# Attention and feed-forward on one core: another hand-written order of the first 28 steps, with GpSimd in it, ten low parts on GpSimd, and first loads from ScalarE's queue

## Chip, cores and metric

One core of one Trainium2 chip. The metric is device time in microseconds (us) of one execution; for the kernel before, the median of three runs is 829.32 us (828.08 to 829.99).

## What is computed

```python
# q, k, v: [8 batches, 8 heads, 576, 64] f32; w_in [512, 2048], w_out [2048, 512] f32
scores = (q @ k^T) / 8
# heads 0-3: key 0..31 places back; heads 4-7: every 4th key, 0..124 places back
attn = softmax(where(mask, scores, -1e9))
x = (attn @ v)  ->  [4608 tokens, 512]
h = x @ w_in
out = (h * clip(h + 3, 0, 6) / 6) @ w_out
```

All of it is float32. For the feed-forward part every operand is split in two: a high part, rounded to the format that TensorE multiplies at full rate, and a low part, which is what the rounding left. A product is three matmuls: high by high, high by low, low by high.

## The kernel before

**Units of work.** Attention is done in 48 trios (half of the heads of a batch by a third of its queries); the first 12 trios belong to the part of the kernel that the change touches. The feed-forward part of the first 1536 tokens is done in chunks of 384 tokens by 16 slices of the hidden 2048. A *step* is one chunk by one slice: a first product of 12 matmuls (128x384) into one of two banks of the pool `ps_h`, a gate on ScalarE and VectorE, and a second product of 9 matmuls (128x512). Chunk 0 needs the trios 0 to 4, chunk 1 the trios 2 to 9. Steps 0 to 2 are chunk 0 by slices 0 to 2; after that chunk 0 (odd step numbers) and chunk 1 (even ones) take turns. The rest of the kernel (other trios, other steps, a Strassen-like product for the later tokens) is laid out by a planner, `_in_time`, and follows behind.

**The weights** come from memory as packed 64-bit words, 32 pieces `w0` to `w31` (two per slice: even ones for the first product, odd ones for the second), and are turned to high and low parts by seven operations: zeroing a sign word on GpSimd (L520, inside `load_w`), two scalings on ScalarE (`U` L531, `Q` L535), two integer operations on VectorE (`j` L539, `a` L546), the high part on ScalarE (`h` L549) and the low part on VectorE (`l` L555).

**What sets the order.** Everything up to step 27 stands in the string `ORDER`, written by hand: each word is an operation and its number, and each engine issues its share of them in that order, waiting in place when something is not ready. `w0@X1` adds a wait: the load of w0 is not issued before X1. The letters:

- `k`, `v`, `M`, `w`: loads of a trio's keys with queries (`load_qk` L206), its values (`load_v` L215), parts of the mask (`load_mask` L812) and a weight piece (L514), all on SP's queue
- `B`: TensorE's scores of a trio (L238, mask L351), together with the products of an earlier trio's weights and values (L248); `V`: such products alone
- `R`, `S` on VectorE (largest value L275, subtraction L279), `X` on ScalarE (exponent L305), `E` turning on TensorE (L374), `CA` its copy by ScalarE (L387)
- `Z` on VectorE (shares, three instructions, L326 to L329), `Y` turning the result on TensorE (L374), `CX` its copy by ScalarE (L391)
- `XH` the high parts of a trio's tokens on ScalarE (L477), `XL` the low parts (L483). A trio that lies in one chunk has one piece (trios 0, 1, 5, 6, 10, 11), the others have three
- `G`, `H`: first and second product of a step (`gemm1` L571 to L573, `gemm2_part` L621 to L623); `RE` on ScalarE (L579) and `T` on VectorE (L582) are the gate; `GH` its high part (`gate_high` L586), `GL` its low part on VectorE (`gate_low` L590)

GpSimd's instructions are not under the hand-written order before: they stand where the builder puts them. `WARM` matmuls on zeros (L173) open the kernel on TensorE.

```python
    with tc.manual_schedule(engines={Activation, DVE, SP}):
        for name in ORDER.split():
            name, _, behind = name.partition("@")
            issued[name] = first_operations[kind](number)   # issues on its engine, in this order
            if behind: ...  # wait for issued[behind]
```

Of the kernel before, what the change touches and what calls it, by code (L numbers as in the profile page):

```python
# [58 lines left out]
XL0 v3@XL0 E2 CA2 Z1 R3 v4@R3 B4 S3 Q0 X3 U0 j0 w2@j0 Y1 CX1 a0 v5@a0 h0 Z2 B6 XH1 R4 Y2 R6 E3 CX2 XL1 k7@CX2 CA3
S6 XH2 B5 S4 X6 w4@XH2 XL2 X4 Q2 l0 E6 U2 Z3 E4 v6@E6 CA6 R5 CA4 Y3 k8@CA6 V4 CX3 S5 XH3 j2 X5 XL3 Q4 E5 Z4 U4 CA5  # L60
a2 Y4 B7 CX4 w6@a2 j4 h2 XH4 l2 k9@j4 B8 Z5 R7 v7@R7 Y5 XL4 CX5 Z6 G0 XH5 S7 Q6 w7@Q6 R8 X7 w1@X7 XL5 Y6 U6 S8 E7
G1 CX6 a4 k10@a4 CA7 v8@CA7 XH6 j6 X8 h4 XL6 B9 w5@G1 RE0 a6 RE1 l4 h6 k11@RE1 T0 E8 Q7 Z7 G2 CA8 GH0 R9 Q1 v9@GH0
GL0 U1 S9 U7 Y7 T1 B10 X9 CX7 l6 GH1 v10@CX7 j1 XH7 E9 G3 R10 RE2 CA9 XL7 Q5 S10 U5 Z8 B11 X10 RE3 a1 GL1 h1 E10 T2
Y8 CA10 Z9 CX8 V10 GH2 R11 XH8 Y9 l1 CX9 Z10 H0 XH9 XL8 XL9 w3@XL8 S11 Y10 G8 GL2 CX10 w16@S11 w13@S11 T3 X11 XH10
GH3 XL10 E11 RE8 GL3 G6 CA11 j5 U3 w28@CA11 T8 Q3 a5 GH8 G10 j7 RE6 w11@GH8 h5 GL8 U16 T6 l5 Q16 Q13 G4 GH6 a7
RE10 Q28 j16 v11@a7 h7 T10 H2 w8@j16 Q11 a16 U28 l7 h16 H3 GH10 GL6 l16 RE4 j3 Q8 w30@RE4 V11 U8 T4 GL10 GH4
G20 w17@U8 Z11 GL4 w9@Z11 a3 Y11 RE20 G13 j28 CX11 h3 T20 XH11 j8 Q30 H4 XL11 U30 l3 w29@Q30 GH20 a8 Q17 a28 U17 H1
GL20 RE13 h8 T13 Q9 j17 GH13 H8 U9 l8 w31@GH20 h28 GL13 Q31 a17 U31 G12 l28 h17 Q29 j9 U29 l17 w14@GL20 G25 Q14
a9 RE12 h9 T12 U14 H20 l9 RE25 GH12 T25 GL12 G5 w15@T25 j14 GH25 j31 GL25 a14 H13 RE5 a31 h14 T5 Q15 l14
U15 H12 j30 GH5 h31 GL5 j15 G18 l31 w23@j14 Q23 a15 a30 h15 G11 RE18 l15 h30 T18 l30 w18@U15 GH18 H10 j29 RE11  # L70
GL18 T11 a29 Q18 G27 GH11 U18 GL11 h29 H18 l29 w19@T18 Q19 RE27 j18 U19 T27 a18 GH27 H25 h18 GL27 l18 w10@Q18
Q10 U10 j19 H11 U11 a19 h19 j10 G22 l19 w12@a19 j11 a10 G15 RE22 a11 h10 T22 h11 l10 GH22 H6 l11 w20@j10 Q12
# [13 lines left out]
def windowed_attention_ffn(ctx: ExitStack, tc: tile.TileContext, qk, vp, w, mask, out, out_t):  # L86
# [100 lines left out]
    def in_turn(ins):

        for name in last.values():
            tc.add_manual_dep(  # L190
                ins.ins, name, mybir.DependencyInfo(mybir.DependencyClass.NoSync, mybir.DependencyReason.DATA), reason="in turn"
            )
# [1404 lines left out]
```

## Time and profile before

| | |
|---|---|
| median of three runs | 829.32 us |
| the profiled execution's own time | 830.10 us |
| its span, first to last instruction | 828.3 us |
| busy in the span: TensorE / weight load | 812.6 / 684.5 us |
| VectorE / ScalarE / GpSimd | 634.7 / 563.4 / 128.5 us |
| HBM read and written | 145.1 and 38.8 MB |

PE is TensorE's matmuls, PEld its weight loads, DVE VectorE, ACT ScalarE, POOL GpSimd, SPq the queue from which transfers are issued. Busy is the union of an engine's instructions. [...] "Idle before, releaser" is an engine's idle time just ahead of an instruction and what ended it. Between the span and the execution's own time lie 1.8 us.

### The profile page before, as it was taken

The page shows a single profiled execution, that of the slowest core. Times are in us where ns is not written, and L with a number is a line of the kernel's source. Part 1 is how long each engine was busy: PE and PEld are TensorE (multiplying, and loading weights), DVE is VectorE, ACT ScalarE, POOL GpSimd, SP SyncE. Part 2 cuts the span into 40 slices and gives each one's busy share as a digit, 9 for nine tenths or more (in the row PEclk, how much of TensorE's full clock was granted, in tenths as well). Part 3 has the DMA queues.
Part 4 walks back from the last instruction along what each step waited for, and adds up shares of the span by engine and source line. Part 5 has one row for each costly group of instructions (what it writes and reads, how often), then busy time and mean ns, then how long its engine had stood idle before and what let it go on. Part 6 is the DMA issues. An engine that isn't in the chain of part 4 may idle for free.

```text
span 828.3 us, 20418 instructions
## 1 busy us (share of the span) xinstructions
PE 812.6 (98%) x8076; PEld 684.5 (83%) x8076; DVE 634.7 (77%) x1131; ACT 563.4 (68%) x1277; POOL 128.5 (16%) x192
## 2 busy tenths in 40 slices
...
GB/s 290 254 205 229 128 103 108 95 170 243 350 215 147 299 299 348 264 366 394 322 263 185 270 147 208 285 224 247 211 121 349 109 235 340 161 174 158 218 138 77
DMA packets 99455, 185.23 MB, mean 224 GB/s; under 512 B 6560, under 2 KB 35232, under 8 KB 99360
## 3 DMA queue, kind: packets, MB, share of 16 engines
...
## 4 chain that ended last, share of the span: by engine, by line
PE 91%; ACT 5%; DMA 1%; DVE 1%; issue 1%; SPq 0%; DVEq 0%; ACTq 0%
PE ps_o L789 27%; PE ps_x L798 8%; PE ps_x L799 8%; PE ps_x L800 8%; PE ps_o L622 5%; PE ps_o L623 5%; PE ps_o L621 5%; PE ps_h L571 5%; PE ps_h L573 5%; PE ps_h L572 5%; PE ps_a L256 2%; PE ps_a L238 2%; DMA first<-in_v 1%; PE ps_b L256 1%; PE ps_b L238 1%
## 5 line engine op out<-in xcount | busy, mean ns | idle before, releaser
L789 PE MATMUL ps_o<-gh,ring 128*128 128x512 f32 x672 | 209.5, 389 | 0.7 <-ACT gh L1252 0.7
L789 PEld LDWEIGHTS ps_o<-gh,ring 128*128 128x128 f32 x672 | 126.1, 188 | 27.7 <-ACT gh L1252 1.5
L798 PE MATMUL ps_x<-cell,ring 128*128 128x512 f32 x336 | 132.5, 394 | 0.0
L789 PE MATMUL ps_o<-gl,ring 128*128 128x512 f32 x336 | 130.9, 390 | 0.6 <-DVE gl L1256 0.6
L799 PE MATMUL ps_x<-cell,ring 128*128 128x512 f32 x336 | 131.0, 390 | 0.0
L800 PE MATMUL ps_x<-cell,ring 128*128 128x512 f32 x336 | 130.8, 389 | 0.0
L1252 ACT CAST gh<-g 128x512 fp32r<-128x512 f32 x168 | 98.5, 620 | 46.1 <-PE ps_o L789 43.4
L1256 DVE TENSOR_TENSOR gl<-g,gh 128x512 fp32r<-128x512 f32 x168 | 109.5, 686 | 19.9 <-ACT gh L1252 9.1
L571 PE MATMUL ps_h<-x,wi 128*128 128x384 f32 x256 | 88.0, 344 | 0.2 <-DVE t L582 0.2
L573 PE MATMUL ps_h<-x,wi 128*128 128x384 f32 x256 | 86.2, 337 | 0.0
L572 PE MATMUL ps_h<-x,wi 128*128 128x384 f32 x256 | 85.9, 335 | 0.0
L623 PE MATMUL ps_o<-wo,gl 128*128 128x512 f32 x192 | 75.8, 395 | 0.0
L622 PE MATMUL ps_o<-wo,gh 128*128 128x512 f32 x192 | 75.6, 394 | 0.0
L621 PE MATMUL ps_o<-wo,gh 128*128 128x512 f32 x192 | 74.8, 389 | 0.3 <-PE ps_a L374 0.3
L789 PEld LDWEIGHTS ps_o<-gl,ring 128*128 128x128 f32 x336 | 63.1, 188 | 14.1 <-DVE gl L1256 1.2
L798 PEld LDWEIGHTS ps_x<-cell,ring 128*128 128x128 f32 x336 | 63.1, 188 | 13.8
L800 PEld LDWEIGHTS ps_x<-cell,ring 128*128 128x128 f32 x336 | 63.1, 188 | 13.3
L799 PEld LDWEIGHTS ps_x<-cell,ring 128*128 128x128 f32 x336 | 63.1, 188 | 12.9 <-DVE cell L773 0.4
L520 POOL TENSOR_SCALAR va<-st 128x512 f32<-128x512 f32 x32 | 53.9, 1688 | 75.0 <-DMA st<-in_w 67.0
L579 ACT ACTIVATE t<-ps_h,three 128x384 f32<-128x384 f32 x64 | 37.2, 583 | 40.4 <-PE ps_h L573 36.6
L302 ACT ACTIVATE e<-e,mx 128x64 f32<-128x64 f32 x216 | 56.6, 345 | 4.7 <-POOL mx L294 4.5
L1221 DVE TENSOR_TENSOR g<-g 128x1024 f32<-128x1024 f32 x48 | 57.4, 1217 | 0.0
...
## 6 DMA issues: line engine op xcount, KB each, us to landing
ring<-sums SPq DMA_DIRECT2D x84, 512.0 KB, 7.6
ring<-rights SPq DMA_DIRECT2D x84, 512.0 KB, 6.5
st<-in_w SPq DMA_DIRECT2D x32, 512.0 KB, 4.0
...
out<-o SPq DMA_DIRECT2D x11, 512.0 KB, 3.4
```

The lines of the kernel that those rows point to most:

```text
L571: nc.tensor.matmul(ph, lhsT=wt(f, 0)[:, ks], rhs=a, start=(kt == 0), stop=False)
L572: nc.tensor.matmul(ph, lhsT=wt(f, 0)[:, ks], rhs=b, start=False, stop=False)
L573: ins = nc.tensor.matmul(ph, lhsT=wt(f, 1)[:, ks], rhs=a, start=False, stop=(kt == NK - 1))
L621: nc.tensor.matmul(po[c][tt], lhsT=gh[:, rows], rhs=wt(f, 2), start=first, stop=False)
L622: nc.tensor.matmul(po[c][tt], lhsT=gh[:, rows], rhs=wt(f, 3), start=False, stop=False)
L623: return nc.tensor.matmul(po[c][tt], lhsT=gl[:, rows], rhs=wt(f, 2), start=False, stop=(f == NF - 1))
L789: nc.tensor.matmul(banks[part], lhsT=right[:, a, cols], rhs=x, start=(start and not i), stop=(i == 2), skip_group_check=True)
L798: nc.tensor.matmul(bank, lhsT=tile_[:, 0, ks], rhs=h[:, kt], start=(start and kt == 0), stop=False, skip_group_check=True)
L799: nc.tensor.matmul(bank, lhsT=tile_[:, 0, ks], rhs=l[:, kt], start=False, stop=False, skip_group_check=True)
L800: nc.tensor.matmul(bank, lhsT=tile_[:, 1, ks], rhs=h[:, kt], start=False, stop=(kt == 1), skip_group_check=True)
L1252: nc.scalar.copy(two[0], gated_tile(g, q, k))
L1256: nc.vector.tensor_tensor(out=two[1], in0=gated_tile(g, q, k), in1=two[0].bitcast(F32), op=ALU.subtract)
```

## The change

1. `ORDER` is another list of the same operations for the first 28 steps. From `j12 G24 a13` on the words are the same as before, and behind them every engine's instructions are the same. Weight slices are taken up in another sequence (w16, w6, w4, w0, w17, w14, ...), and the first steps of TensorE are 13, 2, 3, 0, 11, 1, 4 in place of 0, 1, 2, 3, 8, 6, 10.
2. GpSimd's instructions come under the hand-written order too. The zeroing has a word of its own, `s`; the gate's high parts of 13 steps go from ScalarE to GpSimd (`POOL_HIGHS`); the low parts of ten trios (0 to 3, 5 to 8, 10, 11) are GpSimd's, before of two (10, 11).
3. The loads k0 to k4, v3, M0 and M1 are issued on ScalarE's queue; the others stay with SP. The mask comes in four parts: the first has 32 rows by 896 columns (before 32 by 2560), the second is the 128x128 unit matrix.
4. `WARM` is 7, before 8. Which slice opens an accumulation in the second product is no longer fixed to slice 0. Ordering hints among loads (`in_turn`) are gone, since the list orders them.

```diff
-WARM = 8
+WARM = 7
-POOL_LOWS = frozenset((10, 11))
+POOL_LOWS = frozenset((0, 1, 2, 3, 5, 6, 7, 8, 10, 11))
+POOL_HIGHS = frozenset((2, 3, 6, 8, 10, 12, 13, 14, 17, 18, 19, 22, 26))
+BY_ACT = frozenset(('k0', 'M0', 'k1', 'k2', 'k3', 'k4', 'v3', 'M1'))
 ORDER = """
-k0 M0 M1 k1 k2 v0 k3 v1 B0 k4 v2 R0 S0 B1 X0 R1 E0 S1 CA0 X1 w0@X1 B2 Z0 R2 E1 CA1 k6@CA1 Y0 B3 S2 CX0 k5@S2 XH0 X2
+k0 M0 k1 M1 v0 B0 R0 S0 B1 k2 M2 v1 R1 v2 k3 X0 v4@R1 E0 S1 X1 E1 CA0 B2 k4 R2 CA1 B3 w16@B1 w6@CA0 S2 X2 Z1 Z0 E2
...
+    def queue_of(name):
+        return nc.scalar if name in BY_ACT else nc.sync
...
-            ins = nc.sync.dma_start(out=kqs[t], in_=qk[t].rearrange("h d x -> (h d) x"))
+            return queue_of(f"k{t}").dma_start(out=kqs[t], in_=qk[t].rearrange("h d x -> (h d) x"))
...
+    def cv_zero(p):
         hi_w, _, _, sign = parts(p)
-        nc.gpsimd.tensor_scalar_mul(sign, hi_w, 0.0)
-        return ins
+        return nc.gpsimd.tensor_scalar_mul(sign, hi_w, 0.0)
...
-        first = f == 0
+        if c not in po:
+            begun[c] = n
+        first = begun[c] == n
...
-        (slice(0, QB), slice(0, mask.shape[1])), (slice(QB, P), slice(0, P)), (slice(QB, P), slice(2 * P, mask.shape[1]))
+        (slice(0, QB), slice(P, 2 * P + 2 * CH)), (slice(0, P), slice(0, P)),
+        (slice(0, QB), slice(2 * P + 2 * CH, mask.shape[1])), (slice(QB, P), slice(2 * P, mask.shape[1])),
...
-        "G": gemm1, "RE": relu, "T": gate, "GH": gate_high, "GL": gate_low, "H": gemm2,
+        "s": cv_zero, "U": cv_product, "Q": cv_round, "j": cv_sign, "a": cv_add, "h": cv_high, "l": cv_low,
+        "G": gemm1, "RE": relu, "T": gate, "GH": lambda n: gate_high(n, nc.gpsimd.tensor_copy if n in POOL_HIGHS else nc.scalar.copy), "GL": gate_low, "H": gemm2,
...
-        engines={mybir.EngineType.Activation, mybir.EngineType.DVE, mybir.EngineType.SP}
+        engines={mybir.EngineType.Activation, mybir.EngineType.DVE, mybir.EngineType.SP, mybir.EngineType.Pool}
```

**ScalarE at the start of the program, before** (`e` are exponents, `a` and `xf` the copies CA and CX, `x_87` high parts of tokens):

```order
L305 ACT_TABLE_LOAD
L305 ACTIVATE e<-e 128x384
L387 COPY a<-ps_a 128x384
L305 ACTIVATE e<-e 128x384
L387 COPY a<-ps_a 128x384
L391 COPY xf<-ps_a 128x6x2x32
```

The same place of the changed program (`first` are the tiles of keys and values, `mi` the mask):

```order
L203 DMA first<-in_qk 128x832
L805 DMA mi<-in_mask 32x896
L203 DMA first<-in_qk 128x832
L805 DMA mi<-in_mask 128x128
L203 DMA first<-in_qk 128x832 x2
L299 ACT_TABLE_LOAD
L299 ACTIVATE e<-e 128x384 x2
L380 COPY a<-ps_a 128x384
L203 DMA first<-in_qk 128x832
L380 COPY a<-ps_a 128x384
```

Six loads stand ahead of the table load, X1 now stands ahead of CA0 (the first copy to `a`), and the load of k4 between CA0 and CA1.

**GpSimd from its first zeroing on, before** (`va<-st` is the zeroing, `x<-xf,x` low parts of tokens):

```order
L520 TENSOR_SCALAR va<-st 128x512 x7
L483 TENSOR_TENSOR x_97<-xf,x_91 128x2x192
L520 TENSOR_SCALAR va<-st 128x512 x9
L483 TENSOR_TENSOR x_97<-xf,x_91 128x2x192
L520 TENSOR_SCALAR va<-st 128x512 x16
```

The same engine from there in the changed program (`gh` are the gate's high parts):

```order
L515 TENSOR_SCALAR va<-st 128x512 x3
L476 TENSOR_TENSOR x_93<-xf,x_87 128x2x192 x2
L476 TENSOR_TENSOR x_94<-xf,x_88 128x192
L476 TENSOR_TENSOR x_96<-xf,x_90 128x2x48
L476 TENSOR_TENSOR x_94<-xf,x_88 128x2x48 x2
L476 TENSOR_TENSOR x_96<-xf,x_90 128x2x48
L476 TENSOR_TENSOR x_94<-xf,x_88 128x192
L515 TENSOR_SCALAR va<-st 128x512 x2
L476 TENSOR_TENSOR x_95<-xf,x_89 128x2x192
L515 TENSOR_SCALAR va<-st 128x512 x2
L578 CAST gh<-t 128x384
L515 TENSOR_SCALAR va<-st 128x512
```

The low parts of trios 0 to 3 stand behind the zeroing of w16, w6 and w4; those of trio 5 behind two more, and each zeroing waits for its weight piece to land.

**VectorE of the changed program around T0** (the second `t<-t,ps_h` below; the first is T11, the three rows with `x_98` and `x_96` are XL9):

```order
L574 SCALAR_TENSOR_TENSOR t<-t,ps_h 128x384
L273 TENSOR_TENSOR e<-ps_a,mx 128x384
L476 TENSOR_TENSOR x_98<-xf,x_92 128x2x48
L476 TENSOR_TENSOR x_96<-xf,x_90 128x2x48
L476 TENSOR_TENSOR x_98<-xf,x_92 128x192
L574 SCALAR_TENSOR_TENSOR t<-t,ps_h 128x384
L269 TENSOR_REDUCE mx<-ps_a 128x6
L582 TENSOR_TENSOR gl<-t,gh 128x384
```

T0 is the gate of TensorE's fourth step; its sixth, G1, takes the bank that T0 reads. Of the low parts of the trios 0 to 8, only XL4 is still ahead of this place on VectorE, beside XL9.

## Rows read from the trace of the kernel before

**Rows 1.** The page's busy time of each engine (share of the span, instructions).
```profile
PE 812.6 (98%) x8076; PEld 684.5 (83%) x8076; DVE 634.7 (77%) x1131; ACT 563.4 (68%) x1277; POOL 128.5 (16%) x192
```
**Rows 2.** Busy time by stretch: from:to, length, then busy us (and instructions) of PE, PEld, DVE, ACT, POOL, the granted clock of TensorE as a share, the DMA engines' busy share, GB/s.
```profile
5.00:70.00 65.00, 57.54 (x1346) 47.29 (x1350) 53.42 (x119) 46.81 (x105) 21.97 (x15) 0.95 0.75 252
...
5.00:10.00 5.00, 3.59 (x149) 2.57 (x152) 2.23 (x4) 1.42 (x3) 0.29 (x1) 1.00 1.03 398
70.00:160.00 90.00, 90.00 (x475) 81.34 (x466) 74.73 (x121) 58.52 (x108) 34.14 (x21) 1.00 0.41 133
```
**Rows 3.** The same view for the stretch from R0's start on VectorE to the end of XL9, and for the stretch at the lower clock.
```profile
6.28:55.40 49.12, 41.95 (x1187) 33.67 (x1187) 40.21 (x99) 34.51 (x80) 11.04 (x7) 0.93 0.73 248
17.81:24.64 6.83, 6.69 (x170) 4.96 (x166) 5.54 (x14) 3.90 (x11) 1.54 (x1) 0.50 0.74 220
```
**Rows 4.** Timeline around the first step on chunk 1 (start, us, engine, line, operation): XL8 and XL9 on VectorE, then the first matmul of G8.
```profile
53.50 1.87 DVE L483 TENSOR_TENSOR x<-xf,x 128x192 fp32r<-128x192 f32 x6
...
55.73 0.42 PE L571 MATMUL ps_h<-x,wi 128*128 128x384 f32 x1
```
**Rows 5.** TensorE's pace with nothing to wait for, from the chain of waits (start, us, what): V11 alone and a turn of three; and from the timeline two matmuls of a first product on end.
```profile
69.49 0.87 PE ps_a L248 x46
72.65 0.33 PE ps_a L374 x3
...
82.84 0.33 PE L572 MATMUL ps_h<-x,wi 128*128 128x384 f32 x1
83.01 0.33 PE L573 MATMUL ps_h<-x,wi 128*128 128x384 f32 x1
```
**Rows 6.** VectorE's groups in the first 160 us, shapes apart (count | busy us, mean ns of one | idle before).
```profile
L539 DVE SCALAR_TENSOR_TENSOR va<-va 128x512 uint32<-128x512 uint32 x32 | 23.0, 723 | 5.2 <-POOL va L520 4.0 <-ACT va L531 1.2
L546 DVE CUSTOM_DVE_ANT_0 va<-st,va 128x1024 uint16<-128x1024 uint16 x32 | 22.8, 726 | 0.2
L590 DVE TENSOR_TENSOR gl<-t,gh 128x384 fp32r<-128x384 f32 x28 | 18.5, 659 | 5.1 <-PE ps_o L622 2.6 <-ACT gh L586 2.4
L582 DVE SCALAR_TENSOR_TENSOR t<-t,ps_h 128x384 f32<-128x384 f32 x28 | 15.2, 547 | 3.8 <-ACT t L579 3.7
L555 DVE TENSOR_TENSOR wi<-va,wi 128x512 fp32r<-128x512 f32 x16 | 12.3, 768 | 0.7 <-ACT wi L549 0.5
L329 DVE TENSOR_TENSOR x<-ps_a,z 128x384 f32<-128x384 f32 x12 | 6.7, 558 | 0.4
L275 DVE TENSOR_REDUCE mx<-ps_a 128x6 f32<-128x384 f32 x12 | 6.6, 551 | 7.1 <-PE ps_a L238 7.1
L327 DVE RECIPROCAL z<-z 128x6 f32<-128x6 f32 x12 | 2.3, 192 | 0.4
L483 DVE TENSOR_TENSOR x<-xf,x 128x384 fp32r<-128x384 f32 x4 | 2.2, 551 | 0.7 <-ACT x L477 0.7
L326 DVE TENSOR_SCALAR z<-ps_a 128x6 f32<-128x6 f32 x12 | 2.0, 163 | 2.9 <-PE ps_a L248 2.9
```
**Rows 7.** GpSimd's groups, shapes apart, over the span.
```profile
L520 POOL TENSOR_SCALAR va<-st 128x512 f32<-128x512 f32 x32 | 53.9, 1688 | 75.0 <-DMA st<-in_w 67.0 <-ACT wi L549 4.4 <-DVE va L539 1.4
L586 POOL CAST gh<-t 128x384 fp32r<-128x384 f32 x36 | 27.0, 750 | 110.5 <-DVE t L582 91.6 <-PE ps_o L622 5.0 <-PE ps_h L573 4.6
L483 POOL TENSOR_TENSOR x<-xf,x 128x384 fp32r<-128x384 f32 x4 | 4.5, 1121 | 15.7 <-ACT x L477 15.7
L483 POOL TENSOR_TENSOR x<-xf,x 128x192 fp32r<-128x192 f32 x3 | 2.1, 714 | 2.9 <-ACT x L477 2.9
L483 POOL TENSOR_TENSOR x<-xf,x 128x96 fp32r<-128x96 f32 x2 | 1.1, 560 | 0.3 <-ACT x L477 0.3
```
**Rows 8.** Timeline of VectorE: a low part of a weight with GpSimd at rest; then a sign operation and a low part while GpSimd worked throughout (76.6 to 81.2 us).
```profile
31.30 0.69 DVE L555 TENSOR_TENSOR wi<-va,wi 128x512 fp32r<-128x512 f32 x1 [0.51 <-ACT wi L549]
...
78.28 1.51 DVE L539 SCALAR_TENSOR_TENSOR va<-va 128x512 uint32<-128x512 uint32 x1
79.72 1.14 DVE L555 TENSOR_TENSOR wi<-va,wi 128x512 fp32r<-128x512 f32 x1
80.78 0.55 DVE L590 TENSOR_TENSOR gl<-t,gh 128x384 fp32r<-128x384 f32 x1
```
**Rows 9.** Timeline of the start: SP's issue of v0; ScalarE's table load, X0 and the copy CA0; the products B2 on TensorE; S1 and Z0 on VectorE.
```profile
3.03 0.43 SPq L215 DMA_DIRECT2D first<-in_v  x1
0.71 1.28 ACT L305 ACT_TABLE_LOAD   x1 [0.71 <-PEq L1586]
7.47 0.52 ACT L305 ACTIVATE e<-e 128x384 f32<-128x384 f32 x1 [5.47 <-DVE e L279]
8.69 0.48 ACT L387 COPY a<-ps_a 128x384 f32<-128x384 f32 x1 [0.70 <-PE ps_a L374]
9.46 0.21 PE L248 MATMUL ps_a<-first,a 64*32 64x65 f32 x1 [0.55 <-DMA first<-in_v]
8.28 0.56 DVE L279 TENSOR_TENSOR e<-ps_a,mx 128x384 f32<-128x384 f32 x1
10.88 0.16 DVE L326 TENSOR_SCALAR z<-ps_a 128x6 f32<-128x6 f32 x1 [2.04 <-PE ps_a L248]
```
**Rows 10.** GpSimd's waits in the first 160 us (total us, times, longest), and the weight loads of the first 60 us (KB each, median us from issue to landing).
```profile
POOL va L520 <- DMA st<-in_w: 67.0, 18, 9.3
...
st<-in_w SPq DMA_DIRECT2D x11, 512.0 KB, 4.5
```

More of the change, by code (lines that the diff above doesn't have):

```diff
@@ L57 @@
 ORDER = """
-k0 M0 M1 k1 k2 v0 k3 v1 B0 k4 v2 R0 S0 B1 X0 R1 E0 S1 CA0 X1 w0@X1 B2 Z0 R2 E1 CA1 k6@CA1 Y0 B3 S2 CX0 k5@S2 XH0 X2
[L59 to L72, printed above, removed]
@@ L78 @@
-H21 l27 RE23 T23 GH23 H19 GL23 H23
+k0 M0 k1 M1 v0 B0 R0 S0 B1 k2 M2 v1 R1 v2 k3 X0 v4@R1 E0 S1 X1 E1 CA0 B2 k4 R2 CA1 B3 w16@B1 w6@CA0 S2 X2 Z1 Z0 E2
+k5@E0 Y1 CA2 R3 Y0 s16 U16 Q16 B4 v3@CA2 w4@CA2 CX0 S3 j16 X3 E3 a16 U6 CA3 XH0 h16 Q6 Z2 R4 s6 S4 j6 k6@CX0 s4 k7@Q6
+X4 U4 a6 l16 Y2 B5 h6 B6 Q4 R5 E4 CX1 S5 k8@s6 Z3 j4 a4 X5 E5 v5@h16 CA4 XH1 Y3 k9@U4 V4 CA5 R6 B7 v6@XH1 CX2 CX3 XH2
+S6 w0@S5 X6 Z4 Y4 E6 XH3 CX4 CA6 Z5 XH4 XL0 R7 XL1 S7 v7@R6 Y5 B8 X7 w17@S6 l6 U0 E7 XL4 XL2 XL3 Q0 R8 h4 S8 CA7 G13
@@ new lines @@
+Z6 s0 j0 a0 k10@S6 X8 w2@XL3 Y6 l4 RE13 CX5 w14@R8 XH5 T13 E8 s17 B9 h0 U17 R9 XL5 Z7 s14 s2 U14 S9 j14 G2 G3 CA8 U2
+Q14 Q17 l0 RE2 a14 v8@CX5 Q2 X9 CX6 j17 h14 B10 E9 T2 GH13 a17 Y7 XH6 h17 CA9 GL13 k11@h0 G0 RE3 v9@j14 w7@RE2 Z8 s7
+l14 Y8 j2 Q7 CX7 XL6 w1@j2 XH7 B11 T3 CX8 l17 a2 h2 XH8 G11 RE11 Z9 R10 Y9 H13 GH2 CX9 l2 XL7 T11 XH9 w5@GL13 w30@XH7
+S10 X10 XL8 XL9 RE0 T0 v10@G11 w15@XL9 s5 Q1 G1 U30 U7 RE1 R11 G4 RE4 Q5 G10 s30 Q30 GL2 S11 T1 j7 a7 T4 h7 X11 RE10
+U5 j30 l7 G6 GH3 GL3 T10 RE6 U15 U1 s15 s1 T6 w18@RE4 E11 E10 U18 GH10 GH11 CA11 H3 v11@RE10 w8@E11 G18 w3@GH11 j5 a5
@@ L183, in windowed_attention_ffn @@
     kqs, vs = {}, {}
-    last = {}
     plan = []
[L187 to L192, printed above, removed]
     def w_tile(name, shape, dtype=F32):
@@ L367, in block @@
             pvs[tv] = pv
-        last["block"] = product.ins.name
         return product
@@ L549, in cv_high @@
         ins = nc.scalar.copy(wt(p // 2, p % 2 * 2), parts(p)[2])
-        last["taken"] = ins.ins.name
         return ins
```

39 lines of the change are left out of this document (19 added, 20 removed).

## Prediction

> **What bounds the kernel now.** The page's first part says where to look: TensorE is busy 812.6 of 828.3 us, VectorE 634.7, ScalarE 563.4, GpSimd 128.5 [rows 1]. The change adds no product and takes one warming matmul away, so all it can win is time in which TensorE stands or runs slowly. The view by stretch says where that is. Between 70 and 160 us TensorE is busy 90.00 of 90 us; between 5 and 70 it is busy 57.54 of 65 at a mean granted clock of 0.95 [rows 2]. So the prize is in the first 70 us: 7.5 us of idle time, and what the lower clock costs. [...]
>
> Next, who holds TensorE up there. VectorE's row is the thing to see: from its first attention operation, R0 at 6.28, to the end of XL9 at 55.40 it is busy 40.21 of 49.12 us, while GpSimd works 11.04 us [rows 3]. XL8 and XL9 end at 53.50 + 1.87 = 55.37, and G8, the first step on chunk 1, starts at 55.73 [rows 4]. From there to the end of the hand-written list TensorE has hardly a gap. So the end of this part is: VectorE's start, plus its work up to the operation that is late last, plus its idle time, plus TensorE's work from there on. I price the change by these four.
>
> **The change, part by part.**
>
> *VectorE's list.* In the changed order the operation that is latest in this sense is no longer XL9 but T0: TensorE runs the steps 13, 2, 3, 0, 11, 1, and G1 takes the bank that T0 must first read. Counting VectorE's operations up to XL9 before, and up to T0 now: 12 R become 11, 11 Z become 10, ten low parts become two (XL4, XL9), 5 each of j, a, l become 7 each, 3 T become 5, 2 GL become 1. At the means of [rows 6]: less R 0.55; less Z 0.16 + 0.19 + 0.56 = 0.91; less four low parts of one piece, 4 x 0.55 = 2.20, and four of three pieces, 4 x 0.93 (half of 1.87, [rows 4]) = 3.73; less GL 0.66; more 2 x (0.72 + 0.73 + 0.77) = 4.44 of conversions and 2 x 0.55 = 1.09 of gates. Sum: 2.5 us less work.
>
> *TensorE's list behind it.* Behind G8 before stood 24 first products, G8 included; behind G1 now stand 23, plus two more turns and one more block of values (E10, Y10, V10). A first product is 12 matmuls at 0.17 (82.84 to 83.01), 2.1 us; a turn of three about 0.3; the block 0.87 [rows 5]. That is 2.1 - 0.6 - 0.9 = 0.6 us less.
>
> *GpSimd beside VectorE.* Until T0, GpSimd has 8 zeroings at 1.69 (13.5), four low parts of one piece at 1.12 (4.5), four of three pieces at 0.71 + 2 x 0.56 = 1.83 (7.3) and GH13 and GH2 at 0.75 (1.5): 26.8 us against 11.0, 15.8 more [rows 3, 7]. What that does to VectorE is seen in its timeline: a weight's low part takes 0.69 with GpSimd at rest and 1.14 beside it, a sign operation 1.51 [rows 8], while instructions that read a bank of TensorE keep 0.55 to 0.56 on average [rows 6]. Over the first 160 us the means of j, a and l lie 0.03, 0.04 and 0.08 above 0.69, GL's 0.11 above 0.55 [rows 6, 8]: 32 x 0.15 + 28 x 0.11 = 7.9 us, spread over GpSimd's 53.9 us of zeroing and two low parts of 1.12 [rows 7], 0.14 per us of GpSimd. Upper bound: 15.8 x 0.14 = 2.2 us. Lower: the kinds that suffer are 18 of about 38 us of VectorE's work here (48%), against 89 of 128 us in the first 160 (69%), so 2.2 x 0.70 = 1.5. I take 1.8.
>
> *VectorE's idle time*, 8.9 us before (49.12 - 40.21). The start gets worse: X1 now stands ahead of CA0, and E1 ahead of B2. CA0 began at 8.69; now it waits for S1 (ended 8.84) and X1 (0.53), so 9.4; B2 moves from 9.46 to about 10.4, and VectorE's next operation, R2, needs the whole of B2, some 1.5 us [rows 9]. VectorE then idles from 8.84 to about 12.0, 3.2 us in place of 2.0 (8.84 to 10.88). Behind that the list is denser: Z1, Z0, R3, S3 stand ready in a row, and the first conversions are for a piece whose load is issued right after B1. Later XL4 waits for XH4, ahead of which ScalarE has two copies, X6, XH3, CX4 and CA6; about 1.5 us, an estimate by its row of half-microsecond operations. Ends: 3.2 + 1.5 = 4.7 if nothing else waits, 8.9 + 1.2 = 10.1 if every other wait stays. Neither end is nearer to a row; I take the middle, 7.5, so 1.4 us less.
>
> *Loads and the rest.* The six loads on ScalarE and the table load (1.28) lie ahead of X0, where ScalarE idled 5.47 us [rows 9]. The sixth waits for M0, as B0 does; behind it come at most 0.43 + 1.28 = 1.7 us, against a block, R and S (0.87 + 0.55 + 0.56 = 2.0) until X0 needs the table: nothing, and up to 1.7 if ScalarE's issue were slow, which no row shows. v0 leaves at about 0.7 in place of 3.03, but B2 waited only 0.55 us for it [rows 9], and between 5 and 10 us the DMA engines are full (share 1.03, 398 GB/s, [rows 2]); the same bytes must come before B3. Nothing; ends -0.5 and +0.5. k4's issue, up to 0.43, delays CA1; it lies in the idle time above. ScalarE's 13 copies that leave save it work, but it is not what is late last. The smaller WARM and the free accumulation start: nothing.
>
> Sum: 2.5 + 0.6 + 1.4 - 1.8 = 2.7 us. The profiled execution took 830.1 us, 0.8 above the median 829.3; it becomes 827.4, and the median **826.6**. With the ends of idle time and contention it reaches from 829.3 - 5.8 = 823.5 to 829.3 + 0.3 = 829.6.
>
> **Rivals.**
>
> *The waits stay (B).* [...] Then 2.5 + 0.6 - 2.2 = 0.9: 828.4. For it: the clock fell after the blocks B2 and B3 and the turns between them, and the new list has much the same there. Against: VectorE idled only 1.3 us (6.83 - 5.54) in the slow stretch [rows 3], so the clock was not all of it. About 0.2% (1.7 us) is what a measurement can tell from no change; B lies within.
>
> *GpSimd's queue becomes the bound (C), slower.* GpSimd takes its work in order, and before it waited 67.0 us in all for weight pieces, harmlessly [rows 10]. Now low parts stand behind these waits. G4 needs XL8; ahead of it stands the zeroing of w7, whose load waits for RE2. By TensorE's list some 13 us of work lie between G2 and G1, so RE2 ends near 40; landing 4.5 [rows 10], zeroing 1.7, XL6 1.1, GH2 0.75, XL7 and XL8 3.7: done near 52, and G4 is due near 55. Beyond 3 us of lateness each us goes into the end, and at 7.4 the kernel is slower by more than 0.2%. If two pieces each come one landing time late, 9.0: 9.0 - 3.2 - 2.7 = 3.1 slower, 832.4. Against: each earlier piece has room.
>
> *GpSimd blocks VectorE (D), slower.* If every instruction with two inputs from SBUF grew as the sign operation did (1.51 for 0.69, +120%, [rows 8]) whenever GpSimd works: GpSimd is busy 26.8 of 46.8 us, 57%, so 18 x 0.57 x 1.2 = 12.3 us, less what before paid by that price (22% of the time, some 20 us of such work: 5.4), 6.9 in place of 1.8. Then -2.4: 831.7. [...] Against D: the means of [rows 6] lie only 0.03 to 0.11 above the undisturbed times.
>
> **How the numbers follow.** Forecast 0.57, B 0.26, C 0.10, D 0.07. The forecast's centre and most of its spread are faster by over 0.2%; B is no change; C and D are slower: 0.57, 0.26, 0.17. The range runs from 823.3, the forecast's good end with 0.2 for the loads, to 830.8, which takes in its bad end and B, and leaves out the better part of C and D.
>
> **What would show it.** Right: TensorE's first step on chunk 1 about 2.5 us earlier; VectorE busy about 39.5 of 47 us from R0 to T0, GpSimd about 27; l and GL longer than before in that stretch, R and S not; everything behind shifted. Wrong: T0 done long before G1 starts; low parts on GpSimd as what ends TensorE's waits; a low clock in another place; new idle time of TensorE behind 70 us.

## The result, and the profile after

The changed kernel takes 834.22 us (median of 4 runs, 833.94 to 835.09) against 829.48 for the kernel before: 1.0062 of it, 95% interval 1.0044 to 1.0079. It is 0.6% slower, where 826.6 was forecast. The profiled execution took 834.32 us, its span is 832.1, 3.8 more than before; another 0.4 lies outside the span (2.2 in place of 1.8), where no row tells of it. Three slow executions of more than 1100 us, one each of kernels 5 and 8 below and one of the kernel before, are left out of all medians and ratios.

The page's busy line, beside [rows 1], tells that no engine has more to do that matters: TensorE +0.6, VectorE +1.0, ScalarE -6.5, GpSimd +17.7.

```profile
PE 813.2 (98%) x8075; PEld 684.9 (82%) x8075; DVE 635.7 (76%) x1115; ACT 556.9 (67%) x1264; POOL 146.2 (18%) x221
```

By stretch (from:to, length, busy us and instructions of PE, PEld, DVE, ACT, POOL, granted clock, DMA share, GB/s), beside [rows 2]:

```profile
5.00:70.00 65.00, 54.66 (x1256) 46.24 (x1257) 49.88 (x98) 43.74 (x95) 32.53 (x33) 0.97 0.73 247
5.00:10.00 5.00, 3.96 (x99) 2.92 (x100) 1.26 (x3) 1.81 (x2) 0.29 (x1) 1.00 1.02 368
70.00:160.00 90.00, 89.71 (x534) 79.55 (x533) 76.21 (x121) 56.41 (x106) 41.30 (x31) 1.00 0.42 135
```

TensorE does 2.9 us less in the first 70 us (54.66 against 57.54) and the rest is as before. To see where, cut at the first matmul of the first first product: G13 now, G0 before. First the changed kernel, from R0 (7.99; the window starts at 7.97) to G13 (38.72) and from there to 160, the stretch R0 to the end of T0 of which the prediction spoke, and the stretch at the lower clock:

```profile
7.97:60.97 53.00, 43.65 (x1155) 35.99 (x1155) 42.17 (x86) 35.49 (x81) 25.83 (x28) 0.97 0.75 255
7.97:38.72 30.75, 21.40 (x770) 15.76 (x770) 22.00 (x46) 18.46 (x42) 12.51 (x14) 0.99 0.86 300
38.72:160.00 121.28, 120.99 (x972) 108.58 (x971) 104.09 (x173) 80.42 (x157) 61.32 (x51) 0.99 0.46 148
...
37.87:41.28 3.41, 3.41 (x29) 3.23 (x16) 2.54 (x6) 0.90 (x2) 1.23 (x1) 0.50 0.44 131
```

Then the kernel before, from G0 (33.88) on, and from R0 (6.28) to G0:

```profile
33.88:160.00 126.12, 124.40 (x993) 111.31 (x992) 107.32 (x190) 89.01 (x174) 51.18 (x31) 1.00 0.48 158
6.28:33.88 27.60, 21.94 (x767) 16.44 (x767) 20.83 (x50) 16.32 (x38) 4.64 (x3) 0.88 0.86 288
```

The first first product is 4.84 us later: 1.69 up to the window's start, since R0 comes later, and 3.15 between there and it. In these 3.15 TensorE is busy 0.54 less (21.40 against 21.94) and idle 3.69 more (9.35 against 5.66). Behind it the changed kernel is the better one: TensorE stands 0.3 us up to 160 where before it stood 1.7; the span from there to the end is 1.0 shorter. 4.84 - 1.0 is the 3.8.

**The idle time** is a kind of wait that the prediction did not look at. TensorE's timeline of the changed kernel, the rows whose wait the profile gives to "issue", that is to no semaphore, bank or load that it shows:

```profile
19.96 0.24 PE L242 MATMUL ps_a<-first,a 64*32 64x65 f32 x1 [1.35 <-issue]
...
24.55 0.24 PE L242 MATMUL ps_a<-first,a 64*32 64x65 f32 x1 [0.42 <-issue]
...
30.78 0.53 PE L242 MATMUL ps_a<-first,a 64*32 64x65 f32 x18 [1.58 <-issue]
...
36.77 0.24 PE L242 MATMUL ps_a<-first,a 64*32 64x65 f32 x1 [1.75 <-issue]
```

These waits sum to 5.1 us, in the middle of the blocks B4 and B5, of V4, and at the start of B8. The kernel before has two in its first 60 us, and only the first lies ahead of G0:

```profile
17.24 0.21 PE L238 MATMUL ps_a<-first 64*32 64x64 f32 x1 [1.27 <-issue]
...
49.53 0.21 PE L238 MATMUL ps_a<-kq 64*32 64x64 f32 x1 [0.54 <-issue]
```

5.1 - 1.27 = 3.8 is the whole of the additional idle time (3.69): the other waits, taken together, are no longer than before. What these gaps have in common is seen by counting instructions between them, matmuls and weight loads of the changed kernel:

```profile
19.95:24.54 4.59, 3.09 (x127) 2.29 (x127) 4.36 (x8) 3.58 (x7) 3.52 (x3) 1.00 0.56 197
24.54:30.77 6.23, 3.79 (x127) 2.78 (x127) 5.85 (x12) 4.78 (x12) 1.74 (x3) 1.00 0.94 307
30.77:36.76 5.99, 3.88 (x126) 2.83 (x126) 4.83 (x13) 4.70 (x13) 3.75 (x6) 1.00 0.98 342
```

127 + 127 twice and 126 + 126 once, with the few records that a trace lacks 256. And the DMA queues show one packet of 16 KB of the kind "instruction" 2.3 to 2.6 us ahead of the end of each gap (at 17.65, 22.12, 28.16 and 34.21). The count and the packet are what the trace shows. The theory to test, called the instruction fetch below, is my guess from the two: each such packet brings TensorE its next 256 instructions, and where TensorE has run through the 256 before sooner than they come, it stands.

**The start.** TensorE's first mask matmul; ScalarE's table load, X0, X1 and the copy CA0; VectorE's R0 and R2, beside [rows 3, 9]:

```profile
5.99 0.50 PE L345 MATMUL ps_a<-mi 32*128 32x384 bf16 x1 [1.52 <-DMA mi<-in_mask]
```

```profile
6.33 1.28 ACT L299 ACT_TABLE_LOAD   x1 [6.33 <-DMA mi<-in_mask]
9.17 0.52 ACT L299 ACTIVATE e<-e 128x384 f32<-128x384 f32 x1 [1.56 <-DVE e L273]
11.04 0.52 ACT L299 ACTIVATE e<-e 128x384 f32<-128x384 f32 x1 [1.34 <-DVE e L273]
...
11.47 0.46 ACT L380 COPY a<-ps_a 128x384 f32<-128x384 f32 x1
```

```profile
7.99 0.56 DVE L269 TENSOR_REDUCE mx<-ps_a 128x6 f32<-128x384 f32 x1 [6.74 <-PE ps_a L232]
...
13.81 0.56 DVE L269 TENSOR_REDUCE mx<-ps_a 128x6 f32<-128x384 f32 x1 [2.81 <-PE ps_a L232]
```

M0 is smaller now (56 KB, before 160) and was issued at the same time (1.15 and 1.16), and it lands later: at 5.94 (before 5.03), so that B0 starts at 5.99 (before 5.08). The mask matmul takes 0.50, not 0.33, and the whole block 1.93, not 1.14: by these durations TensorE is at its lower clock, since in the kernel before, within the stretch at a granted clock of 0.50, the same matmul takes 0.49 (at 19.19 and 22.52). The trace's first change of clock is at 10.56, where before it was at 4.16. (The clock column says 1.00 for a stretch ahead of the first change; the durations tell.)

**VectorE**, groups of the first 160 us, beside [rows 6]:

```profile
L540 DVE CUSTOM_DVE_ANT_0 va<-st,va 128x1024 uint16<-128x1024 uint16 x32 | 26.1, 817 | 1.5 <-issue 0.5
L533 DVE SCALAR_TENSOR_TENSOR va<-va 128x512 uint32<-128x512 uint32 x32 | 25.8, 810 | 5.1 <-POOL va L515 5.1
...
L574 DVE SCALAR_TENSOR_TENSOR t<-t,ps_h 128x384 f32<-128x384 f32 x28 | 15.1, 547 | 3.2 <-ACT t L571 3.2
```

a and j cost some 90 ns more each than before, T, which reads a bank of TensorE, the same 547. GpSimd's work at the same moment is what tells: of the changed kernel's a, j and wi's low parts in these 160 us, each one with GpSimd at rest throughout took 695 ns or less; with GpSimd at work throughout they took 1144, 1020 and 877 on average, and T 546.

### The profile page after: what moved, and what is told of

The parts are those of the page before. It is cut to its first block, busy times and chain, and to the rows that moved or that the text cites. A ratio compares the mean times of both kernels' runs of the same rounds, so it can differ in the third digit from the quotient of the medians.

```text
span 832.1 us, 20411 instructions
## 1 busy us (share of the span) xinstructions
PE 813.2 (98%) x8075; PEld 684.9 (82%) x8075; DVE 635.7 (76%) x1115; ACT 556.9 (67%) x1264; POOL 146.2 (18%) x221
## 4 chain that ended last, share of the span: by engine, by line
PE 79%; ACT 4%; DVE 1%; issue 1%; ACTq 0%; DVEq 0%
PE ps_o L783 27%; PE ps_x L792 8%; PE ps_x L793 8%; PE ps_x L794 8%; PE ps_o L616 4%; PE ps_o L617 4%; PE ps_o L615 4%; PE ps_h L563 4%; PE ps_h L565 3%; PE ps_h L564 3%; PE ps_a L250 2%; PE ps_b L250 1%; PE ps_b L232 1%; ACT xf L405 1%; ACT t L1063 1%; PE ps_a L232 1%
## 5 line engine op out<-in xcount | busy, mean ns | idle before, releaser
L515 POOL TENSOR_SCALAR va<-st 128x512 f32<-128x512 f32 x32 | 51.6, 1624 | 40.1 <-DMA st<-in_w 39.0
L578 POOL CAST gh<-t 128x384 fp32r<-128x384 f32 x49 | 36.2, 741 | 125.8 <-DVE t L574 103.7
```

## The experiments

The sixteen were timed beside the kernel before, whose median there was 829.8 to 830.6. The last two columns are of one execution each. "First product" is the start of the first matmul of the first G in the profiled execution (33.88 before, 38.72 changed). "Issue" is the sum of TensorE's waits of that kind in its first 60 us.

| kernel | ratio to before (95%) | median us | first product | issue us |
|---|---|---|---|---|
| changed | 1.0062 (1.0044-1.0079) | 834.22 | 38.72 | 5.1 |
| 1 changed, 11 warming | 1.0074 (1.0056-1.0093) | 835.83 | 40.21 | 5.4 |
| 2 changed, 96 instructions more | 1.0464 (1.0438-1.0489) | 868.28 | 47.28 | 12.7 |
| 3 changed, values first | 1.0057 (1.0038-1.0077) | 835.74 | 40.62 | 4.1 |
| 4 changed, all loads from SP | 1.0022 (1.0005-1.0038) | 831.77 | 35.82 | 0.9 |
| 5 as 4, 8 warming | 1.0036 (1.0017-1.0054) | 833.39 | 41.11 | 2.5 |
| 6 before, 7 warming | 1.0020 (1.0009-1.0032) | 831.82 | 37.54 | 0.5 |
| 7 before, two queues | 1.0029 (1.0014-1.0043) | 832.70 | 38.29 | 1.5 |
| 8 as 5, eight lows back | 1.0045 (1.0030-1.0059) | 834.15 | 38.07 | 1.8 |
| 9 changed, four loads later | 1.0058 (1.0041-1.0076) | 835.31 | 40.33 | 5.0 |
| 10 as 5, the same four | 1.0038 (1.0024-1.0053) | 833.30 | 39.99 | 2.2 |
| 11 as 4, the same four | 1.0051 (1.0033-1.0069) | 834.95 | 37.95 | 3.5 |
| 12 before, 6 and 7 together | 1.0031 (1.0017-1.0044) | 832.41 | 39.38 | 0.3 |
| 13 changed, two loads later | 1.0056 (1.0036-1.0075) | 834.32 | 41.32 | 2.8 |
| 14 as 4, the same two | 1.0025 (1.0009-1.0040) | 832.74 | 38.45 | 2.6 |
| 15 before, eight lows to GpSimd | 1.0035 (1.0021-1.0048) | 832.50 | 35.67 | 3.0 |
| 16 before, three lows to GpSimd | 1.0008 (0.9994-1.0021) | 830.57 | 35.62 | 2.1 |

Of kernels 5, 10 and 11 the profiled execution was a long one (837.15, 838.39 and 837.22), so their first product stands late; those of 9, 13 and 14 lay some 1.8 to 1.9 us above their medians. In 5, 8 and 10 one more gap belongs to the column, 2.66, 1.87 and 2.07 at the first value matmul of B8: the profile puts it down to ScalarE, but the copy CA6 that this matmul reads had ended at 35.3, 33.8 and 34.8, some 2 to 3 us before, and it is again the 256th instruction.

**Is it the instruction fetch? (2)**

```diff
+    for _ in range(48):
+        nc.tensor.matmul(idle[:32, :64], lhsT=zeros[:, :32], rhs=zeros[:, P : P + 64], start=True, stop=True)
```

> The changed kernel with 48 tiny matmuls (32 rows of output, 64 columns) added behind the 7 warming ones, into the idle time before B0. It moves every later instruction of TensorE 96 places down its instruction stream. Four gaps of TensorE without any wait (1.35 in B4, 0.42 in B5, 1.58 in V4, 1.75 in B8, 5.1 us in all) lie exactly 256 instructions apart, each 2.3 to 2.6 us behind the start of a 16 KB packet of the instruction queue. Theory F (these are stalls of the instruction fetch): each gap falls 96 instructions earlier in the list of operations, so the first in E2, Y1, Y0 or the first matmuls of B4, and their sum changes by more than 1 us in one direction, since a fetch that falls due in a stretch of waits or long first products is hidden; the time moves with the sum. Rival (they are waits for data or for banks that the profile doesn't show): the gaps stay at the same operations and the same sum. The tiny matmuls may also raise the clock before B0; the run with 11 warming matmuls is the measure for that part.

The gaps go with the count, as theory F has it, and cost far more than I expected: 34 us. Four of the rows, in the attention of the first 60 us and in the steady part behind 200:

```profile
19.89 0.31 PE L244 MATMUL ps_a<-first,a 64*32 64x65 f32 x1 [4.62 <-issue]
...
34.02 0.44 PE L234 MATMUL ps_a<-first 64*32 64x64 f32 x8 [3.69 <-issue]
...
204.35 0.21 PE L252 MATMUL ps_a<-v,a 64*32 64x65 f32 x1 [2.42 <-issue]
...
238.63 0.24 PE L234 MATMUL ps_a<-kq 64*32 64x64 f32 x1 [2.65 <-issue]
```

Counted in TensorE's stream, its gaps stand at instructions 706, 962 and 1218, where the changed kernel has them too, and at 450, 1730 and 1986, whole groups of 256 away: at the same places of the stream, so at operations 96 instructions earlier in the list. The operations did not keep them. Between 200 and 300 us TensorE, with no wait of the kind there in the changed kernel, is busy 87.84 of 100 us; first this kernel, then the changed one:

```profile
200.00:300.00 100.00, 87.84 (x1519) 78.27 (x1507) 73.88 (x171) 74.24 (x237) 23.09 (x45) 1.00 0.68 217
```

```profile
200.00:300.00 100.00, 99.13 (x1754) 88.05 (x1753) 86.43 (x196) 89.39 (x279) 26.85 (x55) 1.00 0.76 249
```

Over the span the waits of this kind sum to 34.2 us (12.2 + 9.0 + 8.7 + 2.4 + 1.9 by line), in the changed kernel to 5.7: 28.5 of the 34 are theirs. The rest goes with TensorE's own work, busy 821.2 us in place of 813.2. In the steady part two attention blocks of some 190 short instructions stand on end; the kernel before and the changed one happen to have the border of a group between the two blocks, this one has a group that holds nothing but attention. The longest gap at a border was 4.62 us (at 19.89).

**Is it the clock at the start? (1, 5, 6)** Edits: `WARM = 11` and `WARM = 8` (5: with `BY_ACT = frozenset()`) in the changed kernel, `WARM = 7` in the one before.

> The changed kernel with 11 warming matmuls in place of 7, so that TensorE stays busy until the first block B0 (5.99 us) instead of stopping at 4.2; nothing else differs. Theory S (the loss sits on TensorE's own path before its first first product: late loads, half clock until 10.56 us, fetch stalls): the clock is at its upper level before B0 ends, B0 and B1 take about 1.1 and 1.0 us instead of 1.93 each, E0 0.5 instead of 0.86; up to 1.5 us come out at the first product G13, the median falls from 834.2 to about 833. Theory V (the loss is VectorE slowed by GpSimd's work beside it, 2.7 us more busy time up to T0): the start is not what ends the phase, the median stays within 0.4 of 834.2. A third outcome: the 1.5 us are won at B1 and lost again at B3, which waits for its loads.

> The changed kernel with two things undone: all first loads from SP's queue, and 8 warming matmuls instead of 7. With 7 and all loads from SP the first product G13 began at 35.82 and TensorE ran at the lower clock until 21.0 us; with 8, in the kernel before, the clock rose at 4.16. Theory S (start and clock of TensorE): the clock is up before B0, B0 and B1 take about 1.1 each, B2 and B3 1.66 instead of 2.51, so that B3 ends some 4 us earlier than 15.81 if its loads are there, and some of it reaches G13: it begins at 34 to 35.5, the median falls 0.5 to 2 below the run with 7 (831.8), to the kernel before or under it. Theory F (stalls of the instruction fetch take back what a faster start wins, since faster blocks ask for instructions sooner): gaps without a wait come back at instructions 706 to 1474 of TensorE's stream, 1 to 5 us in sum, and the median is 831 to 834. Rival (the eighth warming matmul does nothing): the clock still rises at 21, the median within 0.5 of 831.8.

> The kernel before with 7 warming matmuls instead of 8, as in the change. Theory S: the clock does not rise at 4.16 but much later (10 us or more), B0 to B2 take up to twice as long, and part of it reaches the end: 0.5 to 2.5 us slower than the kernel before. Theory of the prediction (the smaller number does nothing): within 0.4 of it. If TensorE is idle anyway behind a half-clock start, waiting for loads, the clock differs and the time does not.

With 11 the clock rose at 7.26 and B2 ended at 13.07 (13.76 with 7), but a gap of 3.50 without a wait stands in Y5 ahead of B8, and the median is 835.83. With all loads from SP an eighth warming matmul did not raise the clock in the profiled run (first change at 20.86; 21.00 with seven) and gave no time. Only in the kernel before is the seventh against the eighth seen, 0.20%; the turn E0 of that run takes 0.88 (0.52 before), its first change of clock is at 23.48:

```profile
8.74 0.88 PE L374 MATMUL ps_a<-ident,e 128*128 128x128 f32 x3
```

So the smaller WARM is not nothing, but giving it back is no cure here: in kernel 1 the faster start met a longer gap, in kernel 5 the start was no faster.

**Is it the two queues? (4, 7, 12)**

```diff
-BY_ACT = frozenset(('k0', 'M0', 'k1', 'k2', 'k3', 'k4', 'v3', 'M1'))
+BY_ACT = frozenset()
```

Kernel 7 puts the same loads of the kernel before on ScalarE's queue, 12 adds `WARM = 7`.

> The changed kernel with all first loads issued from SP's queue, in the written order k0, M0, k1, M1, v0, ... (0.43 us an issue), none from ScalarE's. In the changed kernel SP issues v0, M2 and v1 beside k0 and M0, and B0 waits 1.52 us for M0 (5.99 instead of 5.08). Theory S (the two queues together put 2.4 MB in flight at once and the first two transfers share the DMA engines with v0, M2 and v1): k0 and M0 land near 5.0, B0 starts 0.5 to 0.9 us earlier, R0 near 7.0, and some of it stays: the median falls by 0.3 to 1. Rival (two queues issue sooner, so the start is no worse for it, and the later start has other causes): B0 starts at 6 or later, later loads come later by the longer queue, and the median rises by 0 to 2 us.

> The kernel before with only the queue of the first loads changed, as in the change: k0, M0, M1, k1 to k4 and v3 from ScalarE's queue, v0, v1, v2 from SP's; order, mask parts, low parts and 8 warming matmuls stay. Theory S (v0 and what else SP issues at once shares the DMA engines with k0 and M0): B0 starts 0.5 to 1.2 us later than 5.08, and 1 to 3 us come out at the end. Rival (it is not the queues but the order behind them): B0 within 0.3 of 5.08, the median within 0.5 of the kernel before. A third way: X0 is late by the table load behind the last issue on ScalarE (9.2 instead of 7.47), 1 to 2 us.

> The kernel before with both small parts of the change and nothing of its order: first loads by two queues and 7 warming matmuls. One by one they cost 0.29% and 0.20%, the whole change 0.62%. Theory P (these two are the change's loss, and the new order with GpSimd's low parts is worth about nothing): 0.4 to 0.6% slower, 833.5 to 835.5 against a kernel before of about 830.4. Theory O (the two share one slack, and the new order costs by itself): 0.2 to 0.35%, 832 to 833.3. A third outcome, below 0.2%, would mean that the two undo each other.

Kernel 4 takes two thirds of the loss away. TensorE's B0 and G13, and VectorE's R0:

```profile
4.41 0.50 PE L345 MATMUL ps_a<-mi 32*128 32x384 bf16 x1
...
35.82 0.42 PE L563 MATMUL ps_h<-x,wi 128*128 128x384 f32 x1
```

```profile
6.41 0.56 DVE L269 TENSOR_REDUCE mx<-ps_a 128x6 f32<-128x384 f32 x1 [5.16 <-PE ps_a L232]
```

B0 starts 1.58 us sooner than with two queues and finds M0 there. In the kernel before, the two queues alone delay it by 2.22 (from 5.08) and cost 0.29%. The trace does not put this on ScalarE's queue alone: in the changed kernel k0 from it and v0 from SP, both issued at 0.7, land at 5.29 and 5.01, where k0 of the kernel before, with no v0 beside it, lands at 4.23. TensorE's B0 in kernel 7:

```profile
7.30 0.33 PE L355 MATMUL ps_a<-mi 32*128 32x384 bf16 x1 [2.40 <-DMA mi<-in_mask]
```

Both small edits together cost 0.31% (0.17 to 0.44), no more than the queues alone: that fits theory O, one shared slack, though the interval does not rule out the lower end of theory P. What is odd in 4 is that it won with TensorE at the lower clock until 21.0 (turns of 0.87 to 0.90, against 0.52 to 0.55 at the higher one): "issue" falls from 5.1 to 0.9, and my guess is that the slower blocks give the fetch its time. So by which way the edit gained is not shown.

**Do three orders matter? (3)** `S1 CA0 X1 B2 E1` for `S1 X1 E1 CA0 B2`, and `Z0 Z1` for `Z1 Z0`.

> The changed kernel with three of its new places undone: CA0 ahead of X1, B2 ahead of E1, and Z0 ahead of Z1, as in the kernel before. Theory S as I put it in the prediction (the swap delays B2 by about 1 us and with it VectorE's next step, R2): B2 starts 0.7 to 1.0 us earlier than 12.10, R2 starts near 13.1 instead of 13.81, G13 starts 0.5 to 1 us earlier than 38.72 and the median falls by 0.3 to 1.0. Rival (B3 and B4 wait for their loads and the fetch anyway): B2 is earlier and B4 is not; the median stays within 0.3 of 834.2.

B2 began at 11.02 (12.10), but at the lower clock, which rose only at 19.04, and ended at 13.73 (13.76): nothing came of it. Whether it would at the higher clock stays open.

**Is it GpSimd's work beside VectorE? (8, 15, 16)** Edits: `POOL_LOWS` back to (10, 11) in kernel 5; all ten in the kernel before; (5, 7, 8, 10, 11) there.

> The same as the run with all loads from SP and 8 warming matmuls, and also the low parts of eight trios back on VectorE (GpSimd keeps two, as in the kernel before). Theory V (GpSimd's work beside VectorE is what costs): j, a and l lose much of their 0.1 to 0.2 us each, and the kernel is 1 us or more faster than the run it is built on, although VectorE has 0.55 to 0.93 us more for each low part. Theory S: VectorE is the second in line in this part, with 5.9 us more work it ends T0 and the low parts later, TensorE waits, and the kernel is 0.5 to 4 us slower than the run it is built on. No difference (within 0.5) would mean that VectorE does not end anything here.

> The kernel before with one part of the change alone: the low parts of trios 0 to 3 and 5 to 8 on GpSimd as well (ten in all); order, queues and warming stay. GpSimd takes them in its own queue behind the zeroings, each of which waits for its weight piece. Theory V, the main term of my prediction (VectorE's list up to the last late operation bounds the first 60 us): VectorE has 0.55 x 4 + 0.93 x 4 = 5.9 us less to do before XL9, contention gives 1 to 2 back, the kernel is 1 to 3 us faster (0.1 to 0.4%). Theory S (TensorE's own stalls and clock bound the head, VectorE only the few waits behind it): within 0.2% of the kernel before. Rival C (low parts stuck behind a zeroing that waits for its piece): first products wait for XL1 to XL3 on GpSimd, 2 us or more slower.

> The same with only the low parts of trios 5, 7 and 8 on GpSimd (beside 10 and 11): those that stand last ahead of the first step on chunk 1, where GpSimd has nothing to do between 47 and 57 us. Theory V: G8 starts 0.5 to 1.5 us earlier than 55.73 and that much comes out at the end. Theory S: within 0.2%. Rival C is weak here, since the zeroings ahead of them are done by 47 us.

No: 5.9 us more work for VectorE changes kernel 5 by 0.1%, inside the intervals (1.0036 and 1.0045). On the order before, eight low parts on GpSimd cost 0.35%, and three, chosen where GpSimd stands idle, give nothing. In the profiled execution of kernel 15 the gap in B4 is 2.65 in place of 1.27 and G0 is 1.79 later. TensorE's G0 and G8 in kernel 16:

```profile
35.62 0.42 PE L571 MATMUL ps_h<-x,wi 128*128 128x384 f32 x1
...
56.17 0.42 PE L571 MATMUL ps_h<-x,wi 128*128 128x384 f32 x1
```

From G0 to G8 it needs 20.55 us where the kernel before needs 21.85 (33.88 to 55.73, [rows 4]). But that does not make this piece VectorE's. G0 was 1.74 later in this execution (a gap of 2.10 in B4 in place of 1.27), and where G0 is late the piece is short with VectorE's list unchanged too: 20.86, 20.72 and 20.47 in kernels 6, 7 and 12, while kernel 15, with eight low parts less on VectorE, needs 21.71. G8 of kernel 6, to be set against its G0 at 37.54:

```profile
58.40 0.42 PE L571 MATMUL ps_h<-x,wi 128*128 128x384 f32 x1
```

The waits of TensorE between G0 and G8 in the kernel before (total us, times, longest) name VectorE nowhere, and G8 itself starts without one:

```profile
PE ps_a L238 <- issue: 0.5, 1, 0.5
PE ps_a L248 <- DMA first<-in_v: 0.5, 1, 0.5
PE ps_o L621 <- PE ps_a L374: 0.3, 1, 0.3
PE ps_a L248 <- ACT a L387: 0.2, 1, 0.2
```

Kernel 16's median is that of the kernel before.

**Does the fetch wait behind data? (9, 10, 11, 13, 14)** 9 to 11 move `w6@CA0` to `w6@CA2`, `w4@CA2` to `w4@Y0`, k9 to k10's place and k10 behind v8; 13 and 14 move `w17@S6` to `w17@R8` and `k10@S6` to `k10@E8`.

> The changed kernel with four loads issued later and nothing else: w6 behind CA2 (16.7 us instead of 12.1), w4 behind Y0 (about 18 instead of 16.7), k9 in the place of k10 (31.5 instead of 24.8), k10 behind S9 (about 44 instead of 31.5). Theory D (the instruction fetch is late because its packet stands behind data: from the first instruction of a group of 256 to the start of the next packet pass 3.6 us at 13.5, 3.6 at 24.6 and 3.4 at 30.8, where the DMA engines are 0.95 to 0.98 busy, and 1.0 at 36.8): the packets of the stalls in B4 and V4 start 1 to 2 us sooner, these two stalls (1.35 and 1.58) lose 1 to 2.5 us together, G13 begins 1 to 2.5 us earlier than 38.72 and the median is 831.5 to 833.5. Rival (the delay is the fetch's own, whatever the data): the stalls stay within 0.3 and the median within 0.5 of 834.2, or it is slower by late pieces. A half way: the stall in B8 grows by what V4's loses, since k9 now falls into 31 to 35 us; median 833 to 835.

> The same four later loads, on the changed kernel with all first loads from SP and 8 warming matmuls (833.5). Theory D: 1 to 3 us less, 830.5 to 832.5, at the kernel before or just behind it. Rival: within 0.5 of 833.5.

> The same four later loads, on the changed kernel with all first loads from SP and 7 warming matmuls, which had only one stall (0.88 in B9) before the first 50 us and 831.8. Theory D: the little that is left can come out, 830.5 to 831.8, and if the clock stays low until 21 us no more than that. Rival (the order has no more to give, whatever the loads): within 0.4 of 831.8.

> The changed kernel with two loads issued later: w17 behind R8 (38.9 us instead of 31.1) and k10 behind E8 (42.9 instead of 31.5), out of the stretch in which the fetch for instruction 1474 (first matmuls of B8) waits: from 30.78, when the group before it is begun, to its packet at 34.21 pass 3.4 us, where in idle stretches 1.0 to 1.2 pass. Theory D: its packet starts near 32.5 to 33.2, the stall in B8 falls from 1.75 to 0 to 0.8, G13 begins 1 to 2 us earlier than 38.72; if the fall of the clock at 37.87 belongs to this stall it goes too, another 1.1. Median 831.5 to 833.2. Rival (v6, w0 and v7 alone fill the engines as long): stall and median as they were, 834.2 within 0.5. Loss if a moved load is then late for B10 or the conversion of piece 17: above 834.7.

> The same two later loads on the changed kernel with all first loads from SP and 7 warming matmuls (831.8; no stall in B8 there, one of 0.88 in B9). Theory D: the stall in B9 goes or shrinks, 830.3 to 831.5, level with the kernel before. Rival: within 0.5 of 831.8.

Half of theory D fits the rows, and the useful half did not hold. In kernel 9 the DMA engines were only 0.25 busy from 15 to 20 us; the packet for B4's group started 1.2 us after the group before was entered (3.6 in the changed kernel) and B4 had no gap:

```profile
15.00:20.00 5.00, 4.65 (x106) 3.27 (x101) 3.52 (x11) 2.25 (x5) 1.54 (x1) 0.50 0.25 84
```

But B5, V4 and B8 then stood 1.03, 1.30 and 2.29. In kernel 13 the engines were still 0.93 busy from 30 to 35, the packet for B8 started 5.5 us after its group's forerunner was entered, and the gap grew from 1.75 to 2.57:

```profile
31.03 0.53 PE L242 MATMUL ps_a<-first,a 64*32 64x65 f32 x18 [0.19 <-issue]
...
38.90 0.24 PE L242 MATMUL ps_a<-first,a 64*32 64x65 f32 x1 [2.57 <-issue]
```

None of the five is faster than the kernel it was built on by more than the intervals (11 is 0.3% slower). In kernels 9 and 13 a stall that was taken away in one block came back, longer, in a later one. (The clock of 0.50 in 9 and 13 from 8 to 22 us and longer also had its part in B4, so this is no clean proof that data delays the fetch.)

No version beat the kernel before.

## Why the prediction was wrong

**The step that failed is the first one: who bounds the first 60 us.** I took VectorE's list and idle time up to one landmark as the end of this part, -2.5 and -1.4 us, because the low part of trio 9 ends 0.36 us ahead of G8. But TensorE did not wait for it: between G0 and G8 none of its waits names VectorE, and ahead of G0 VectorE ended only 1.7 us of them, ahead of G13 in the changed kernel 2.2. First the kernel before, then the changed one:

```profile
PE ps_a L374 <- DVE x L329: 1.7, 3, 0.7
```

```profile
PE ps_a L367 <- DVE x L323: 1.8, 3, 1.1
...
PE ps_a L367 <- DVE z L320: 0.4, 1, 0.4
```

Ahead of the first first product TensorE is held by its own start, its clock and the gaps at borders of 256 instructions, and there the change lost 4.84 us. Kernels 8, 15 and 16 say that work taken from VectorE brings nothing in time, in either order.

**The landmark T0 before G1 did not exist.** I let G1 wait for T0. G1's first matmul starts at 59.85, T0 only at 60.42, so G1 does not take the bank that T0 reads, as I had it when I described the change; T11, which reads the other one, had ended at 58.87:

```profile
59.85 0.33 PE L563 MATMUL ps_h<-x,wi 128*128 128x384 f32 x1
```

```profile
60.42 0.54 DVE L574 SCALAR_TENSOR_TENSOR t<-t,ps_h 128x384 f32<-128x384 f32 x1
```

The sign of being right did not come either: G4, the first step on chunk 1, starts at 61.96, 6.2 later than G8 before, with two more first products (4.2 us) ahead of it.

**"The loads on ScalarE: nothing" failed.** I counted ScalarE's issue time against its idle time, which held, and did not ask what the earlier v0, M2 and v1 do to the two transfers that B0 needs. They land later: B0 0.91 us later, R0 1.7 later than before. Alone, in the kernel before, it costs 0.29%.

**"The smaller WARM: nothing" failed** for the kernel before (0.20% alone); with the two queues it adds nothing that the intervals show.

**X1 ahead of CA0** was seen rightly in kind and undersized: B2 at 12.10 in place of 10.4, R2 at 13.81 in place of 12.0, which is no more than the late start. Undoing it gave nothing.

**The idle time** of VectorE from R0 to T0's end was 10.8 us (53.00 - 42.17), not 7.5, and above the worse end of 10.1.

**The contention** was 4.5 us, not 1.8, by difference: VectorE is busy 42.17 us from R0 to T0's end, where 39.5 with 1.8 of it were forecast. a, j and the low parts of weights grew to 817, 810 and 815 to 842 ns on average. That instructions which read a bank of TensorE are untouched held (T 547). Neither the idle time nor the contention can have cost TensorE much, since the waits that VectorE ended grew only from 1.7 to 2.2 us.

**TensorE's list behind it**: forecast -0.6; from the first first product to the end the changed kernel is 1.0 shorter.

**The rivals.** B was nearest in kind, a start that loses what the order wins, with a second stretch at a clock of 0.50 (37.87 to 41.28); its price, 0.9 faster, left out the new idle time. C did not occur: the low part XL3 on GpSimd ends at 33.46 and G13 waited for B8 on TensorE; XL8 ended at 59.89, not near 52, but G4 was due only at 61.96 and did not wait. D's growth, 6.9 us, came to 4.5, and its effect did not come. The 1.27 us of "issue" in B4 stood in the trace of before and just ahead of the fall of the clock at 17.81 that I counted as a prize; I passed over it because nothing was named that it waited for.

What stays open: with both small parts undone the new order still costs 0.36%, with GpSimd's low parts undone as well 0.45%. The runs don't separate how much of this is these gaps and how much waits and clock; no run takes the gaps away and leaves the rest as it was.
